# Sign bits of the split weights by a 16-bit operation with one source, and 128 small matmuls at the end of attention and MLP on one core

## The chip, the cores and the metric

The kernel runs on one core of a Trainium2 chip. The core has a matrix engine (PE; its weight loads are shown as PEld), three engines that work on up to 128 partitions at a time (DVE, ACT, POOL), and SP, whose queue here issues all transfers. The metric is the device time of one execution in microseconds; less is better.

## The reference

```python
# q, k, v: 4 batches, 8 heads, 768 positions, 64 wide; block 32, window 16
k_sum = k.reshape(B, H, 24, 32, D).max(axis=3)
v_sum = v.reshape(B, H, 24, 32, D).mean(axis=3)
local = where(abs(i - j) < 16, scale * q @ k.T, -1e9)
far   = scale * q @ k_sum.T + log(32)
a     = softmax(concat([local, far], axis=-1))
x     = (a @ concat([v, v_sum], axis=2))          # to 3072 rows x 512
h     = x @ w_in                                  # 512 -> 2048
out   = maximum(0.01 * h, h) @ w_out              # 2048 -> 512
```

Each query sees the keys nearer than 16 positions and 24 block summaries; then every row goes through a two-layer MLP. Inputs and output are fp32.

## The kernel before

**Work and tiles.** The 3072 rows are eight chunks of 384 rows (three row blocks of 128). Attention of a chunk is 12 units, one row block for one pair of heads. A unit makes scores on PE (`scores`, L328: fp32, 64 rows of contraction, 64 queries and 120 keys at a time), the lowest and the exponentials on DVE and ACT (L333, L340), normalizes on DVE, transposes on PE (`turn`, L345), copies on ACT, multiplies by the values on PE (`values`, L351), and splits the result into a rounded and a rest part `x` (hi on ACT, lo on DVE). In chunk 0 the units run singly, later in pairs; a pair's scores, values and transposes of different ages form a "group" on PE, named `s_('g', n, ...)` and `to_('g', n, ...)`. The block means of v (`vsum`) are reduced on DVE (L222) and then spread by transfers (L282); the maxima of k are reduced on DVE too (L206).

**The MLP in split precision.** Matmuls run on fp32r operands in three terms: hi by hi, lo by hi, hi by lo. For each of 16 slices f of the hidden width, `m1` (L585) makes 12 matmuls of 384 columns into `h`, ACT makes `gs` and `ghi`, DVE `glo`, and `m2` makes 9 matmuls of 512 columns (L604 to L606) into the accumulators `a`.

**The weights.** They come as 64-bit floats, since the host does no arithmetic on them, in 32 tiles of 128 by 512 (w_in and w_out of each slice). `weights` turns a tile `raw` into a hi and a lo part in six steps. `s0` (L538, DVE) shifts the low words right by 29, which leaves three mantissa bits. `s1` (L541, DVE) puts the sign bit of the high word into the low word. `s2` (ACT) scales the high word's exponent. `s3` (L547, DVE) shifts the high word left by three and ors it into the low word, which is then the fp32 value. `s4` (L550, ACT) rounds it to `win_hi` or `wout_hi`, and `s5` (L553, DVE) subtracts to `win_lo` or `wout_lo`. All of DVE's steps go over 512 elements at a step of 8 bytes, except for what the last one writes. The slices of the weights are prepared once, and all eight chunks use them.

**What sets the order.** `Plan` is a list scheduler. Every operation has an engine, a cost (for DVE `65 + 1.042 n` ns, or `65 + 0.52 n` when it is called fast), a priority (a due time, with tuned offsets in tables), and dependencies, including those of the buffers. `order` takes, engine by engine, the ready operation with the lowest priority, and the result is written out with a manual schedule: it is the order of each engine's instructions and of SP's transfers. Before PE's first MLP work, wherever the plan leaves PE idle for over 300 ns, dummy matmuls on a zero tile fill the gap (`spare`, L695).

**The end.** After the last slice three accumulators are copied out by ACT, DVE and ACT (L619, L617), and SP issues three stores of 256 KB (L622). L745 is the end of the program, at which all engines meet.

Of the kernel before, what the change touches and what calls it, by code (L numbers as in the profile page):

```python
# [8 lines left out]
F32 = mybir.dt.float32  # L9
F32R = mybir.dt.float32r  # L10
BF16 = mybir.dt.bfloat16
I32 = mybir.dt.int32
AF = mybir.ActivationFunctionType
ALU = mybir.AluOpType
AX = mybir.AxisListType
# [122 lines left out]
def ACT(n, psum=False, extra=0):  # L138
    return (51 if psum else 93) + 0.833 * n + 93 * extra


def DVE(n, fast=False):
    return 65 + (0.52 if fast else 1.042) * n
# [6 lines left out]
def build(tc, ctx, a):  # L150
    nc = tc.nc
    pool = lambda name, bufs: ctx.enter_context(tc.tile_pool(name=name, bufs=bufs))
    psum = lambda name, bufs: ctx.enter_context(tc.tile_pool(name=name, bufs=bufs, space=bass.MemoryType.PSUM))
    cst = pool("cst", 1)
    st = pool("st", 2)
    ps_acc, ps_h, ps_s, ps_t = psum("pacc", 1), psum("ph", 2), psum("pss", 1), psum("pst", 1)
# [19 lines left out]
    P = Plan()  # L176
    tl = {}
    first = {}

    def load_op(name, prio, fn, **kw):  # L180
        first[name] = P.op("SP", 550, prio, fn, **kw)
        return first[name]

    def new(tag, key, shape, dt=F32, bufs=2, src=None):
        tl[key] = (src or st).tile(shape, dt, tag=tag, name="_".join(str(x) for x in key), bufs=bufs)
        return tl[key]
# [115 lines left out]
    def place(u, at=None):  # L302
        c = min(u // UPC, NCH - 1) if at is None else at
        t, d = PLACE.get(c, (UPC * c, 1.0))
        return t + d * (u - UPC * c)
# [31 lines left out]
    def expo(u, h):  # L337
        e, m, z = tiles_of(u // 2)
        n = 2 * (u % 2) + h
        nc.scalar.activation(out=e[:, n], in_=e[:, n], func=AF.Exp, scale=-1.0, bias=m[:, n:n + 1], accum_out=z[:, n:n + 1])  # L340

# [178 lines left out]
    def weights(f, w, t):  # L520
        if w:
            hi, lo = wout_hi[:, f], wout_lo[:, f]
            shape = lambda x: x
        else:
            hi, lo = win_hi[:, :, 128 * f:128 * f + 128], win_lo[:, :, 128 * f:128 * f + 128]
            shape = lambda x: x.rearrange("p (k f) -> p k f", k=4)
        kr = ("raw", f, w)

        def load():
            nc.sync.dma_start(out=new("big", kr, [128, 1024], bufs=BIG).bitcast(I32), in_=a["w"][f, w].bitcast(I32))  # L530

        lw = lambda: tl[kr].rearrange("p (n t) -> p n t", t=2)[:, :, 0]
        hw = lambda: tl[kr].rearrange("p (n t) -> p n t", t=2)[:, :, 1]
        li = lambda: tl[kr].bitcast(I32).rearrange("p (n t) -> p n t", t=2)[:, :, 0]
        hi_i = lambda: tl[kr].bitcast(I32).rearrange("p (n t) -> p n t", t=2)[:, :, 1]

        def s0():
            nc.vector.tensor_scalar(out=li(), in0=li(), scalar1=29, scalar2=None, op0=ALU.logical_shift_right)  # L538

        def s1():  # L540
            nc.vector.scalar_tensor_tensor(out=li(), in0=hi_i(), scalar=-2 ** 31, in1=li(), op0=ALU.bitwise_and, op1=ALU.bitwise_or)  # L541

        def s2():
            nc.scalar.mul(hw(), hw(), 2.0 ** -112)  # L544

        def s3():
            nc.vector.scalar_tensor_tensor(out=li(), in0=hi_i(), scalar=3, in1=li(), op0=ALU.logical_shift_left, op1=ALU.bitwise_or)  # L547

        def s4():
            nc.scalar.copy(hi, shape(lw()))  # L550

        def s5():
            nc.vector.tensor_tensor(out=lo, in0=shape(lw()), in1=hi.bitcast(F32), op=ALU.subtract)  # L553
        o = load_op(("w", f, w), t - 0.25 * BIG, load, alloc=[("big", kr, BIG)], size=128 * 4096, rate=380.0)
        o = P.op("DVE", DVE(512, True), t + 0.05, s0, after=[o], use=[kr])
        o = P.op("DVE", DVE(512), t + 0.1, s1, after=[o], use=[kr])
        o = P.op("ACT", ACT(512), t + 0.1, s2, after=[o], use=[kr])
        o = P.op("DVE", DVE(512), t + 0.12, s3, after=[o], use=[kr])
        o = P.op("ACT", ACT(512), t + 0.3, s4, after=[o], use=[kr])
        w_op[f, w] = [o, P.op("DVE", DVE(512), t + 0.4, s5, after=[o], use=[kr])]  # L560
# [4 lines left out]
    def gnew(tag, key):  # L565
        n = turns[tag]
        turns[tag] += 1
        x = f"{tag}{n % 2}"
        if n < 2:
            gap(GGAP[n + 2 * (tag == "glo")], st, x)  # L570
        return new(x, key, [128, T], F32R, bufs=1)


    def mlp(c, f0, f1, t0):
# [13 lines left out]
        def gs(f):  # L588
            nc.scalar.activation(out=new("gs", G("gs", f), [128, T], bufs=1), in_=tl[G("h", f)][:, :T], func=AF.Prelu, alpha=0.01)  # L589

        def ghi(f):
            nc.scalar.activation(out=gnew("ghi", G("ghi", f)), in_=tl[G("h", f)][:, :T], func=AF.Prelu, alpha=0.01)  # L592

# [62 lines left out]
    for c in range(NCH):  # L656
        b, cb = divmod(c, CPB)
        for p in range(NP):
            t = place(TPC * (c * NP + p))
# [6 lines left out]
        for p in range(NP):  # L666
            t = place(TPC * (c * NP + p))
            operands(c, p, t, 0 if c else 7 - 2.5 * p)
    for f in range(NF):
        for w in range(2):  # L670
            weights(f, w, LEAD - WT + min(f, SPL) * WS + max(f - SPL, 0) * WS2 + WO * w + (W0 if f == 0 else 0))
# [4 lines left out]
    t = LEAD  # L676
# [9 lines left out]
    zero = cst.tile([128, 128], BF16, name="zero")  # L686
    nc.vector.memset(zero, 0.0)
    spare = ps_acc.tile([128, 512], F32, tag="a2", name="spare")
    with tc.manual_schedule():
        until, begun = 900.0, False  # L690
        for o in todo:
            if o["eng"] == "PE" and not begun:
                begun = o.get("mlp", False)
                while until < o["at"] - FGAP:
                    nc.tensor.matmul(spare[:, :128], zero[:, :128], zero[:, :128], start=True, stop=True)  # L695
                    until += 107 if until < WARM else 57
                until = o["at"] + o["cost"]
            o["fn"]()


def layouts(q, k, v, moe_w_in, moe_w_out):
# [47 lines left out]
```

## Time and profile before

| | |
|---|---|
| Runs (3) | 655.44, 656.45, 658.07 us; median 656.45 |
| Profiled execution | 655.79 us, its span 654.0 us |
| PE busy | 643.3 us (98%), granted clock 0.999 |
| DVE, ACT, POOL busy | 283.5, 298.4, 4.2 us |
| DMA | 58.08 MB, mean 89 GB/s |

The span runs from the first to the last instruction; what the time has beyond it lies around the program. Busy time is a mean over stages of very different kinds, so the prediction reads it by stretches. Ends of matmuls are modelled, and matmuls overlap, so that the distance between starts tells more than a matmul's own duration. A row of instructions has the engine, the line, the operation, what it writes and reads, its shape and its count; then busy us, mean ns of one, and the engine's idle time before them.

### The profile page before, as it was taken

What the parts mean: (1) busy time and instruction counts of PE and PEld (TensorE: products, weight loads), DVE (VectorE), ACT (ScalarE), POOL (GpSimd) and SP (SyncE); (2) the same over time, 40 slices, a digit from 0 to 9 for tenths busy, and PEclk for the clock granted to TensorE, in tenths of its full rate; (3) what the DMA queues carried; (4) which work ended last, traced back from release to release, by engine and by line L of the source; (5) the groups of instructions that cost most, each with busy time, mean ns of one, the idle gap of its engine ahead of it and who ended that gap; (6) DMA issues with size and microseconds to landing.
All of it is one profiled execution on the core that took longest, in us unless ns stands there. A gap on an engine that the chain in (4) does not pass through costs nothing.

```text
span 654.0 us, 11675 instructions
## 1 busy us (share of the span) xinstructions
PE 643.3 (98%) x4582; PEld 559.4 (86%) x4582; DVE 283.5 (43%) x931; ACT 298.4 (46%) x894; POOL 4.2 (1%) x10
## 2 busy tenths in 40 slices
PE   8899999999999999999999999999999999999997
PEld 5588788898888998888888888888888888889996
DVE  5999999933575212223353423242233323211111
ACT  5898776733655313444434443353443434222112
POOL 0200000000000000000000000000000000000000
PEclk9999999999999999999999999999999999999999
DMA  8977577601754000211334220020111100010001
GB/s 313 280 237 243 187 228 238 182 1 46 202 166 140 5 1 24 73 37 52 99 91 122 60 61 26 26 94 24 35 36 35 62 24 1 1 50 1 1 1 48
DMA packets 27207, 58.08 MB, mean 89 GB/s; under 512 B 3024, under 2 KB 13328, under 8 KB 27152
## 3 DMA queue, kind: packets, MB, share of 16 engines
q1 hardware_dynamic: 27152, 57.33, 28.8%
q8 instruction: 36, 0.59, 0.4%
q14 instruction: 19, 0.16, 0.1%
HBM read 48.97 MB, written 6.29 MB: 84 GB/s over the span
## 4 chain that ended last, share of the span: by engine, by line
PE 89%; DVE 5%; DMA 3%; ACT 2%; issue 1%; SPq 0%; ACTq 0%
PE h L585 39%; PE a L605 13%; PE a L604 13%; PE a L606 13%; DMA raw<-in_w_dram 1%; DMA v<-vsum 1%; ACT e L340 1%; PE spare L695 1%; DVE raw L547 1%; DVE raw L541 1%; DMA kn<-in_k_dram 1%; DVE wout_lo L553 0%; PE o L351 0%; DVE e L333 0%; DVE glo L595 0%
## 5 line engine op out<-in xcount | busy, mean ns | idle before, releaser
L585 PE MATMUL h<-x,win_hi 128*128 128x384 f32 x1024 | 263.8, 338 | 0.0
L595 DVE TENSOR_TENSOR glo<-gs,ghi 128x384 fp32r<-128x384 f32 x128 | 71.2, 557 | 285.1 <-ACT gs L589 285.0
L585 PEld LDWEIGHTS h<-x,win_hi 128*128 128x128 f32 x1024 | 186.0, 188 | 9.7 <-issue 0.2
L592 ACT ACTIVATE ghi<-h 128x384 fp32r<-128x384 f32 x128 | 62.7, 490 | 266.1 <-PE h L585 265.7
L585 PE MATMUL h<-x,win_lo 128*128 128x384 f32 x512 | 173.0, 338 | 1.0 <-DVE win_lo L553 1.0
L604 PE MATMUL a<-wout_hi,ghi 128*128 128x512 f32 x384 | 153.5, 400 | 0.0
L605 PE MATMUL a<-wout_lo,ghi 128*128 128x512 f32 x384 | 151.8, 395 | 0.0
L606 PE MATMUL a<-wout_hi,glo 128*128 128x512 f32 x384 | 151.3, 394 | 0.0
L585 PEld LDWEIGHTS h<-x,win_lo 128*128 128x128 f32 x512 | 96.0, 188 | 1.6 <-DVE win_lo L553 1.6
L606 PEld LDWEIGHTS a<-wout_hi,glo 128*128 128x128 f32 x384 | 72.2, 188 | 16.9
L605 PEld LDWEIGHTS a<-wout_lo,ghi 128*128 128x128 f32 x384 | 72.3, 188 | 11.6 <-DVE wout_lo L553 0.4
L604 PEld LDWEIGHTS a<-wout_hi,ghi 128*128 128x128 f32 x384 | 72.1, 188 | 11.6
L340 ACT ACTIVATE e<-e,m 128x120 f32<-128x120 f32 x192 | 73.9, 389 | 5.5 <-DVE m L333 5.1
L589 ACT ACTIVATE gs<-h 128x384 f32<-128x384 f32 x128 | 62.2, 486 | 1.7 <-PE h L585 1.1
L340 ACT ACTIVATION_READ_ACCUMULATOR e<-e,m 128x1 f32 x192 | 36.7, 191 | 0.0
L479 DVE TENSOR_TENSOR e<-e,z 128x480 f32<-128x480 f32 x42 | 27.5, 655 | 0.9
L273 ACT COPY k<-kn 128x288 f32<-128x288 f32 x64 | 24.4, 433 | 4.6 <-DMA kn<-in_k_dram 4.6
L544 ACT ACTIVATE raw<-raw 128x512 f32<-128x512 f32 x32 | 21.7, 691 | 9.2 <-DVE raw L541 9.1
L541 DVE SCALAR_TENSOR_TENSOR raw<-raw 128x512 int32<-128x512 int32 x32 | 22.2, 698 | 0.0
L547 DVE SCALAR_TENSOR_TENSOR raw<-raw 128x512 int32<-128x512 int32 x32 | 21.4, 684 | 0.4 <-ACT raw L544 0.3
L471 DVE TENSOR_SCALAR z<-z 128x4 f32<-128x4 f32 x42 | 7.0, 168 | 33.3 <-ACT e L340 33.3
L206 DVE TENSOR_REDUCE ksum<-kn 128x24 f32<-128x768 f32 x16 | 15.2, 948 | 8.1 <-DMA kn<-in_k_dram 8.1
(588 smaller groups left out, 493.3 us busy)
## 6 DMA issues: line engine op xcount, KB each, us to landing
raw<-in_w_dram SPq DMA_DIRECT2D x32, 512.0 KB
v<-in_v_dram SPq DMA_DIRECT2D x32, 288.0 KB
kn<-in_k_dram SPq DMA_DIRECT2D x16, 400.0 KB
k<-in_q_dram SPq DMA_DIRECT2D x32, 192.0 KB
out_dram<-out SPq DMA_DIRECT2D x21, 256.0 KB
vb<-in_vb_dram SPq DMA_DIRECT2D x12, 384.0 KB
kn<-in_k_dram SPq DMA_DIRECT2D x16, 208.0 KB
v<-vsum SPq DMA_DIRECT2D x24, 72.0 KB
```

Source lines behind the costliest of these rows:

```text
L273: nc.scalar.copy(k, x)
L340: nc.scalar.activation(out=e[:, n], in_=e[:, n], func=AF.Exp, scale=-1.0, bias=m[:, n:n + 1], accum_out=z[:, n:n + 1])
L479: nc.vector.tensor_tensor(out=e, in0=e, in1=z.unsqueeze(2).broadcast_to([128, 4, LK]), op=ALU.mult)
L541: nc.vector.scalar_tensor_tensor(out=li(), in0=hi_i(), scalar=-2 ** 31, in1=li(), op0=ALU.bitwise_and, op1=ALU.bitwise_or)
L547: nc.vector.scalar_tensor_tensor(out=li(), in0=hi_i(), scalar=3, in1=li(), op0=ALU.logical_shift_left, op1=ALU.bitwise_or)
L585: nc.tensor.matmul(h[:, :T], w[:, k, 128 * f:128 * f + 128], x[:, k], start=n == 0, stop=n == 11)
L589: nc.scalar.activation(out=new("gs", G("gs", f), [128, T], bufs=1), in_=tl[G("h", f)][:, :T], func=AF.Prelu, alpha=0.01)
L592: nc.scalar.activation(out=gnew("ghi", G("ghi", f)), in_=tl[G("h", f)][:, :T], func=AF.Prelu, alpha=0.01)
L595: nc.vector.tensor_tensor(out=gnew("glo", G("glo", f)), in0=tl[G("gs", f)], in1=tl[G("ghi", f)].bitcast(F32), op=ALU.subtract)
L604: nc.tensor.matmul(o, gh, wout_hi[:, f], start=f == f0, stop=False)
L605: nc.tensor.matmul(o, gh, wout_lo[:, f], start=False, stop=False)
L606: nc.tensor.matmul(o, gl, wout_hi[:, f], start=False, stop=f == f1 - 1)
```

## The change

Two edits. In `s1` an operation with two sources on 32-bit words becomes one with a single source on 16-bit words: it takes the upper half of the high word, keeps its top bit, and writes it to the upper half of the low word, which is zero after `s0`. The plan is given the fast cost for it. At the end, behind all planned work, PE makes 128 fp32 matmuls of a zero tile `zw` by itself in eight shapes into the two banks that `h` used; nothing reads the results. `zw` is cleared on DVE at the start.

```diff
         def s1():
-            nc.vector.scalar_tensor_tensor(out=li(), in0=hi_i(), scalar=-2 ** 31, in1=li(), op0=ALU.bitwise_and, op1=ALU.bitwise_or)
+            w16 = tl[kr].bitcast(I16).rearrange("p (n t) -> p n t", t=4)
+            nc.vector.tensor_scalar(out=w16[:, :, 1], in0=w16[:, :, 3], scalar1=-2 ** 15, scalar2=None, op0=ALU.bitwise_and)
...
         o = P.op("DVE", DVE(512, True), t + 0.05, s0, after=[o], use=[kr])
-        o = P.op("DVE", DVE(512), t + 0.1, s1, after=[o], use=[kr])
+        o = P.op("DVE", DVE(512, True), t + 0.1, s1, after=[o], use=[kr])
...
     nc.vector.memset(zero, 0.0)
     spare = ps_acc.tile([128, 512], F32, tag="a2", name="spare")
+    zw = cst.tile([128, 128], F32, name="zw")
+    nc.vector.memset(zw, 0.0)
...
             o["fn"]()
+
+        end = [ps_h.tile([128, 512], F32, tag="h", name=f"end{i}") for i in range(2)]
+        for rows, cols, n, count in ((64, 64, 120, 16), (64, 64, 88, 16), (64, 32, 88, 32), (128, 64, 64, 8), (128, 64, 32, 16), (128, 32, 32, 16),
+                                     (64, 64, 24, 16), (64, 128, 24, 8)):
+            for i in range(count):
+                r, c = i % (128 // rows), i // (128 // rows) % (128 // cols)
+                nc.tensor.matmul(end[r][cols * c:cols * c + cols, :n], zw[rows * r:rows * r + rows, :cols], zw[rows * r:rows * r + rows, :n], start=True, stop=True)
```

The new cost changes the plan, and with it the order on PE, DVE, ACT and SP as long as weights are prepared. In what follows, the line numbers after the change are one to three higher. A name's number tells buffers apart.

On DVE, the third weight tile, `raw_0_389`, before (its `s1` is L541, its `s0` stands earlier):

```order
L541 SCALAR_TENSOR_TENSOR raw_0_389<-raw_0_389 128x512
L288 COPY k_1_520<-ksum_1_177 128x6x24
L538 TENSOR_SCALAR raw_0_454<-raw_0_454 128x512
L541 SCALAR_TENSOR_TENSOR raw_1_368<-raw_1_368 128x512
L471 TENSOR_SCALAR z_619<-z_619 128x4
L541 SCALAR_TENSOR_TENSOR raw_0_454<-raw_0_454 128x512
```

And after (`raw_0_373`; `s0` is now L539, `s1` L543, `s3` L549):

```order
L539 TENSOR_SCALAR raw_0_373<-raw_0_373 128x512
L382 RECIPROCAL z_511<-z_511 128x2
L543 TENSOR_SCALAR raw_0_373<-raw_0_373 128x512
L386 TENSOR_TENSOR e_509<-e_509,z_511 128x240
L378 TENSOR_SCALAR z_511<-z_511 128x2
L539 TENSOR_SCALAR raw_0_450<-raw_0_450 128x512
L382 RECIPROCAL z_511<-z_511 128x2
L549 SCALAR_TENSOR_TENSOR raw_0_373<-raw_0_373 128x512
```

Before, this tile's sign step stood behind the four L333 of group 6, at row 122 of DVE's order; now it stands ahead of them, at row 110, and its `s3` follows at row 115, where it stood at row 133.

On PE, around the scores and transposes of group 7 (L328 and L345), before; `h_0` and `h_1` belong to the first and second slice:

```order
L328 MATMUL s_('g', 7, 1)_721<-k_1_520 64x120 x2
L328 MATMUL s_('g', 7, 1)_722<-k_1_520 64x120 x2
L345 MATMUL to_('g', 7, 1)_723<-ident,e_617 120x128 x4
L585 MATMUL h_0_605<-x_80,win_hi 128x384
L585 MATMUL h_0_605<-x_84,win_hi 128x384
L585 MATMUL h_0_605<-x_80,win_lo 128x384
L585 MATMUL h_1_759<-x_80,win_hi 128x384
```

And after, with L587 for L585, L329 for L328 and L346 for L345:

```order
L587 MATMUL h_1_717<-x_80,win_lo 128x384
L587 MATMUL h_0_598<-x_80,win_hi 128x384
L587 MATMUL h_0_598<-x_84,win_hi 128x384
L587 MATMUL h_0_598<-x_80,win_lo 128x384
L329 MATMUL s_('g', 7, 1)_738<-k_0_399 64x120 x2
L329 MATMUL s_('g', 7, 1)_739<-k_0_399 64x120 x2
L329 MATMUL s_('g', 7, 1)_738<-k_1_538 64x120 x2
L329 MATMUL s_('g', 7, 1)_739<-k_1_538 64x120 x2
L346 MATMUL to_('g', 7, 1)_740<-ident,e_660 120x128 x4
L587 MATMUL h_1_717<-x_80,win_hi 128x384
```

Nine of the 12 matmuls of the second slice and the last three of the first moved ahead of group 7; the second slice's last three stay behind it. The dummies L695 go from 154 to 150.

At PE's end, before, the program ends behind the last slice's matmuls:

```order
L605 MATMUL a_0_1_6220<-wout_lo,ghi_15_6620 128x512
L606 MATMUL a_0_1_6220<-wout_hi,glo_15_6624 128x512
L604 MATMUL a_0_2_6224<-wout_hi,ghi_15_6620 128x512
L605 MATMUL a_0_2_6224<-wout_lo,ghi_15_6620 128x512
L606 MATMUL a_0_2_6224<-wout_hi,glo_15_6624 128x512
L745 UNCONDITIONAL_BRANCH
```

After, these rows stand among the new ones (L709), where the shape goes from 64x32 tiles over 128x64 and 128x32 back to 64x64:

```order
L709 MATMUL end_6642<-zw 32x88
L709 MATMUL end_6643<-zw 32x88
L709 MATMUL end_6642<-zw 64x64 x8
L709 MATMUL end_6642<-zw 64x32 x16
L709 MATMUL end_6642<-zw 32x32 x16
L709 MATMUL end_6642<-zw 64x24
L709 MATMUL end_6643<-zw 64x24
```

Where a tile takes 64 rows of contraction, the two halves of the rows alternate and write to two banks; where it takes 128, all go to one bank. None of the new matmuls waits for anything but the last readers of the banks of `h`.

More of the change, by code (lines that the diff above doesn't have):

```diff
@@ L12 @@
 I32 = mybir.dt.int32
+I16 = mybir.dt.int16
 AF = mybir.ActivationFunctionType
```

## The prediction

> **What bounds the kernel now.** I read the page's totals and its slices first, then busy time by stretches, then who waited for whom, and last the order of time at the start and at the end.
>
> ```profile
> span 654.0 us, 11675 instructions
> PE   8899999999999999999999999999999999999997
> DVE  5999999933575212223353423242233323211111
> PE 89%; DVE 5%; DMA 3%; ACT 2%; issue 1%; SPq 0%; ACTq 0%
> L541 DVE SCALAR_TENSOR_TENSOR raw<-raw 128x512 int32<-128x512 int32 x32 | 22.2, 698 | 0.0
> L538 DVE TENSOR_SCALAR raw<-raw 128x512 int32<-128x512 int32 x32 | 13.1, 424 | 0.2 <-DMA raw<-in_w_dram 0.2
> ```
>
> ```profile
> core 0: us, PE busy (x) PEld busy (x) DVE busy (x) ACT busy (x) POOL busy (x), PEclk, DMA share, GB/s
> 16.00:24.00 8.00, 6.83 (x73) 3.08 (x74) 7.57 (x28) 5.87 (x25) 2.65 (x4) 1.00 0.99 287
> 24.00:32.00 8.00, 7.40 (x123) 5.31 (x124) 7.67 (x41) 7.48 (x32) 0.83 (x1) 1.00 0.94 268
> 32.00:44.00 12.00, 11.48 (x119) 9.81 (x117) 11.62 (x42) 11.10 (x36) 0.00 (x0) 1.00 0.76 224
> 44.00:118.00 74.00, 71.81 (x546) 61.79 (x546) 72.97 (x186) 56.33 (x142) 0.00 (x0) 1.00 0.74 226
> 118.00:650.00 532.00, 532.00 (x3589) 470.27 (x3586) 174.49 (x593) 208.58 (x632) 0.00 (x0) 1.00 0.18 53
> 650.00:654.00 4.00, 0.18 (x1) 0.00 (x0) 0.19 (x1) 0.58 (x1) 0.00 (x0) 0.82 0.53 197
> ```
>
> There are three stages. From 118 to 650 us PE is busy all the time, so nothing on DVE can move that part. From 16 to 118 DVE is busy almost without a break (72.97 of 74 us in the largest stretch), and PE has gaps or runs the dummy matmuls of L695. After 650 PE has nothing to do and the last rows leave. The change touches the second stage (L541, the sign step, 32 times) and the third (new matmuls). Only two things count: how much earlier PE becomes saturated, and whether the new matmuls outlast the end.
>
> The profiled execution took 655.79 us for a span of 654.0, so 1.8 us lie around it. The median of the runs is 656.45, or 0.66 above it. I make the sum on the span and put the difference onto the median. About 0.5%, 3.3 us, is what a measurement of this kernel can tell from no change.
>
> **The sign step.**
>
> ```profile
> 34.01 0.42 DVE L538 TENSOR_SCALAR raw<-raw 128x512 int32<-128x512 int32 x1
> 34.35 0.68 DVE L541 SCALAR_TENSOR_TENSOR raw<-raw 128x512 int32<-128x512 int32 x1
> 34.95 0.16 DVE L471 TENSOR_SCALAR z<-z 128x4 f32<-128x4 f32 x1
> ```
>
> The busy time of L541 alone, by stretches:
>
> ```profile
> 0.00:44.00 44.00, 4.52 (x6) 1.00 0.87 276
> 44.00:118.00 74.00, 14.31 (x21) 1.00 0.74 226
> 118.00:160.00 42.00, 3.41 (x5) 1.00 0.21 65
> ```
>
> L538 has one source and the same 512 elements at a step of 8 bytes; the next instruction starts 0.34 us after it. After L541, which has two sources, it starts 0.60 us later. The new step has one source and steps of 8 bytes, on 16-bit elements. No row shows a 16-bit operation, so its bounds are 0.60 (no gain) and, were it twice as fast as L538 again, 0.17. I take 0.34, since L538 is its nearest neighbour in all but the width of the element.
> The Trainium skill, "VectorE: DVE Perf Modes", section "What auto-detection actually checks", says that a single source in SBUF gives two elements a cycle, and four only if every tensor is 16-bit with a step of one. The step here is four elements, so by that page the 0.17 is out; no run here shows it yet.
>
> Each step saves 0.26 us: 6 of them by 44 us, or 1.6 us (the row's 4.52 us for six holds one slow one, which could add 0.4); 21 more by 118, another 5.5; the last 5 lie where PE is saturated, and are worth nothing. What of that reaches PE?
>
> ```profile
> PE h L585 <- DVE win_lo L553: 1.0, 2, 0.5
> PE s_('g', 14, 2)_1690 L351 <- DMA v<-vsum: 0.9, 1, 0.9
> PE t L345 <- ACT pt L396: 0.9, 1, 0.9
> PE to_('g', 11, 1)_1128 L345 <- DVE e L479: 0.8, 1, 0.8
> ```
>
> Up to 44 us DVE decides when the weights are ready, and the dummies stand in PE's way only as filling, so I take the 1.6 in full. After 44 PE has 74 - 71.81 = 2.2 us of gaps to lose, whatever DVE saves. Of these the wait for e (0.8) hangs on DVE, and the wait for vsum's transfer (0.9) starts behind DVE reductions; I take 1.3. The sum is -2.9 us. The ends are 0 (the transfers hold the start: DMA share 0.99 and 0.94 up to 32 us; ACT is next in line with 7.48 of 8 us) and -5.5 (2.6 at the start, were each step 0.17, all of the 2.2, and 0.7 of waits at matmuls that count as busy).
>
> The planner has the new price too, so it writes another order on all engines. On PE, nine matmuls of the second slice of w_in now stand ahead of the scores and transposes of group 7, which stood ahead of them before; they need win_lo of that slice, whose DVE operation moves up as well. If that comes late, the scores wait behind it, and with them DVE and ACT. Dummies go from 154 to 150, worth 0.3 us at most where nothing else waits (11 of them took 0.72 us in the chain, below). The loads on SP's queue change places by one to three; their buffers come free earlier with DVE, so they go out earlier, into transfers that are dense up to 32 us. I put the reordering at 0, between -1 and +2.
>
> ```profile
> 7.79 0.72 PE spare L695 x11
> ```
>
> The memset of zw on DVE costs nothing: DVE waits 4.9 us there for the first keys, and a memset of half as many words took 0.11 us.
>
> ```profile
> 0.82 0.11 DVE L687 MEMSET zero<- 128x64 uint32 x1 [0.82 <-PEq L739]
> 5.83 0.95 DVE L206 TENSOR_REDUCE ksum<-kn 128x24 f32<-128x768 f32 x1 [4.90 <-DMA kn<-in_k_dram]
> ```
>
> **The 128 matmuls at the end.** First the room for them.
>
> ```profile
> 649.42 1.73 SPq L622 DMA_DIRECT2D out_dram<-out  x3
> 649.54 0.40 PE L605 MATMUL a<-wout_lo,ghi 128*128 128x512 f32 x1
> 649.78 0.40 PE L606 MATMUL a<-wout_hi,glo 128*128 128x512 f32 x1
> 650.21 0.58 ACT L619 COPY out<-a 128x512 f32<-128x512 f32 x1 [0.82 <-PE a L606]
> L745 SPq EVENT_SEMAPHORE  x7: 17/28/28, 653.0 to 653.9; - x7
> L745 SPq DRAIN  x3: 7/7/7, 653.3 to 653.6; - x3
> L745 PEldq DRAIN  x2: 13/1333/2653, 647.6 to 653.6; - x2
> ```
>
> PE's queue drains at 647.6 + 2.65 = 650.2. SP waits for the last store until 653.0, works off its waits until its own drain at 653.3, and then all engines meet, 0.7 us before the end. So PE may work until 653.3 at no cost. The new matmuls start at 650.0 (649.78 and the step from the one before, 0.24), with 3.3 us of cover. What do they take? Each fp32 matmul is two instructions in the trace, so there are 256.
>
> ```profile
> 60.29 0.27 PE L328 MATMUL s_('g', 10, 1)_1036<-k 64*64 64x120 f32 x2
> 60.30 0.27 PE L328 MATMUL s_('g', 10, 1)_1037<-k 64*64 64x120 f32 x2
> 60.39 0.27 PE L328 MATMUL s_('g', 10, 1)_1036<-k 64*64 64x120 f32 x2
> 60.50 0.27 PE L328 MATMUL s_('g', 10, 1)_1036<-k 64*64 64x120 f32 x2
> 60.71 0.69 PE L351 MATMUL s_('g', 10, 1)_1036<-pt,v 120*64 120x64 f32 x16
> 61.33 0.65 PE L345 MATMUL to_('g', 10, 1)_1038<-ident,e 128*120 128x128 f32 x4
> 61.73 0.59 PE L585 MATMUL h<-x,win_hi 128*128 128x384 f32 x2
> ```
>
> In 64x64 tiles four instructions run side by side (_1037 starts 10 ns after _1036), and a round for 120 columns takes 0.10 us. L351 (128x64, two tiles) makes 16 in 0.62 us with a change of shape; without it about 0.06 a round. L345 loads 120 columns of weights for 0.10 us each (4 to the next group in 0.40). A change of shape costs 0.14: the round at 60.50 is 0.21 long in place of 0.10, and the next group's first is longer too.
>
> By shape: 64x64 with 120 columns, 8 rounds of 0.10, 0.8; with 88 columns, 8 of 0.075, 0.6; 64x32 with 88, 8 rounds if all eight tiles go together, 0.6; 128x64 with 64, 8 of 0.06, 0.5; with 32 columns, 16 rounds that the weights hold at 0.06, 0.9; 128x32, 8 of 0.03, 0.3; 64x64 with 24, 8 of 0.06, 0.5; 64x128, 8 of 0.11, 0.9. That is 5.1, and six changes of shape make 5.9 us. The low end is 4.2 (rounds by columns alone, no load in the way); the high end is L351's mean for all 256, 39 ns each, 10 us.
>
> So PE ends at 650.0 + 5.9 + 0.2 = 656.1, and then follow 0.7 us (the barrier alone) to 1.0 (SP's waits as well); with 0.9 that is 657.0, or +3.0 us. The ends are +1.3 and +7.
>
> **Sum.** +3.0 - 2.9 = +0.1 us on the profiled execution, 655.9; on the median, 656.5.
>
> **Rivals.**
> - The tail is covered. If the tiles of a round start as close as the scores' do (10 ns) in all shapes, 256 instructions at 13 ns each take 3.3 us and nothing shows; with 3.9 us won in front in place of 2.9, that is 656.5 - 3.0 - 1.0 = 652.5. For it speaks that close start; against it, the 0.10 us from round to round and the 39 ns of L351. It decides from a front gain of 3.3 us on.
> - A slow tail. If the rounds don't form over eight tiles or in the narrow shapes, L351's 39 ns makes +7: 656.5 + 4 = 660.5. In the densest 8 us of the table PE made 123 matmuls, 65 ns each, waits included; were that what it can issue in a long run, 256 take 16.6 us, and the time is 667. Sixteen in 0.62 us speak against that, unless they had been queued ahead. It decides from 36 ns an instruction on (a tail of 9.1 us).
> The Trainium skill, "TensorE: Matmul & The Clock Gate", section "Wait — 56ns, not 53.3ns?", puts the issue at about 62 ns a matmul when the sequencer decodes in software; by that, an estimate, 256 are 15.9 us. The sixteen in 0.62 us don't bear it out for short runs; no run here shows a long one.
> - The 16-bit operation isn't fast. At 0.60 us DVE saves nothing, and only the tail is left, 656.5 + 2.9 = 659.4. Since the planner then counts on time that DVE doesn't have, some waits of PE can come on top, 660.5.
> - The new order brings new waits: group 7 behind the second slice's win_lo, at 0.5 us for each such wait as in the row of win_lo. Three or four of them eat the gain: 659 to 660.
>
> **How the numbers follow.** My forecast, 653.5 to 659, has 0.57; the covered tail, with its gain, 0.17; the slow tail 0.13; the 16-bit operation at full price 0.07; the bad order 0.06. Faster by over 0.5% (under 653.2) is the second case and a sliver of the first, 0.18; slower (over 659.7) is the slow tail and half of the last two, 0.20; the rest is 0.62. The range takes in the covered tail and the price of a slow operation: 652.4 to 660.5.
>
> **What would show it.** The sign step's group should have a mean near 0.42 us, as L538 has. DVE should have visible gaps before 118 us, and PE's waits for win_lo, e and vsum should be shorter. PE's matmuls of the second slice of w_in should start some 2 us earlier than before. The tail should run from about 647 to 653 and end last in the chain. A tail under 3.3 us, or one of over 10, or a sign step of 0.68 would make me wrong, and so would a gain of over 5 us before 118.

## The result, and the profile after

The changed kernel takes 661.27 us (median of 9 runs, 660.72 to 662.80) against 656.45 for the kernel before on the same chip: a ratio of 1.0063, with a 95% interval of 1.0038 to 1.0088. It is slower by 0.6%; the forecast was 656.5 with a range up to 660.5. The ratio is not the quotient of the two medians, which is 1.0073; the nine executions of the kernel before in this comparison took 655.39 to 661.38. The profiled execution took 661.15 us for a span of 659.4 (before: 655.79 and 654.0).

From the page of the changed kernel: the head, the slices of PE and DVE, the chain by engine, and the group of the new sign step; then, from the groups on the tile `raw`, durations as minimum, median and maximum.

```profile
span 659.4 us, 12173 instructions
PE   9899899999999999999999999999999999999999
DVE  5999999913575212232254332332233233111111
PE 83%; DVE 8%; DMA 6%; ACT 2%; issue 1%; SPq 0%
L543 DVE TENSOR_SCALAR raw<-raw 128x512 int16<-128x512 int16 x32 | 23.9, 753 | 0.0
```

```profile
L539 DVE TENSOR_SCALAR raw<-raw x32: 398/429/693, 12.5 to 128.8; 128x512 int32<-128x512 int32 x32
L543 DVE TENSOR_SCALAR raw<-raw x32: 717/752/815, 13.0 to 129.8; 128x512 int16<-128x512 int16 x32
```

The sign step does not have the 0.42 us of the shift next to it. Its mean is 753 ns, where the operation that it replaces had 698. DVE stays as full as it was, and its share of the chain goes from 5% to 8%. Stretches of the changed kernel, with the columns that the prediction showed:

```profile
44.00:118.00 74.00, 69.51 (x532) 58.71 (x531) 72.26 (x188) 55.27 (x144) 0.00 (x0) 1.00 0.71 222
118.00:650.00 532.00, 532.00 (x3588) 470.33 (x3587) 173.76 (x592) 208.79 (x632) 0.00 (x0) 1.00 0.18 54
650.00:660.00 10.00, 8.37 (x266) 7.13 (x264) 0.69 (x1) 1.17 (x2) 0.00 (x0) 1.00 0.23 82
```

PE was to lose its gaps between 44 and 118 us. It lost busy time instead: 69.51 in place of 71.81 us, 2.3 us less. From 118 to 650 it is full as before, so what is lost by 118 is lost for good. What PE waited for (total, times, longest) (the first three rows are new):

```profile
PE to_('g', 12, 1)_1256 L346 <- ACT win_hi L552: 1.6, 1, 1.6
PE to_('g', 13, 2)_1586 L346 <- DVE e L480: 1.0, 1, 1.0
PE to_('g', 14, 2)_1683 L346 <- ACT ghi L594: 0.9, 1, 0.9
PE h L587 <- DVE win_lo L555: 0.8, 2, 0.6
```

And the end, with the last matmul of the second layer and the new matmuls of L709:

```profile
651.71 0.40 PE L608 MATMUL a<-wout_hi,glo 128*128 128x512 f32 x1
652.04 6.44 PE L709 MATMUL end<-zw 64*64 64x120 f32 x256
651.35 1.74 SPq L624 DMA_DIRECT2D out_dram<-out  x3
```

The last matmul of the second layer starts at 651.71 us (649.78 before): 1.9 us are lost in front. From there to the end of the span it is 7.66 us (4.23 before): 3.4 us are lost behind. Together that is the 5.4 us by which the span grew, from one profiled execution to the other.

### The profile page after: what moved, and what is told of

Same layout as the page of the kernel before. It is cut to its first block, busy times and chain, and to the rows that moved or that the text cites. A ratio compares the mean times of both kernels' runs of the same rounds, so it can differ in the third digit from the quotient of the medians.

```text
span 659.4 us, 12173 instructions
## 1 busy us (share of the span) xinstructions
PE 650.5 (99%) x4834; PEld 565.4 (86%) x4834; DVE 282.4 (43%) x932; ACT 297.6 (45%) x894; POOL 4.1 (1%) x10
## 4 chain that ended last, share of the span: by engine, by line
PE 83%; DVE 8%; DMA 6%; ACT 2%; issue 1%; SPq 0%
PE h L587 36%; PE a L606 12%; PE a L607 12%; PE a L608 12%; DMA vb<-in_vb_dram 2%; DVE raw L543 2%; DMA v<-in_v_dram 1%; DVE raw L549 1%; DMA raw<-in_w_dram 1%; DVE wout_lo L555 1%; PE end L709 1%; DVE win_lo L555 1%; DMA kn<-in_k_dram 1%; DVE raw L539 1%; DVE glo L597 1%
## 5 line engine op out<-in xcount | busy, mean ns | idle before, releaser
L587 PE MATMUL h<-x,win_hi 128*128 128x384 f32 x1024 | 263.7, 338 | 0.0
L587 PEld LDWEIGHTS h<-x,win_hi 128*128 128x128 f32 x1024 | 186.0, 188 | 9.7 <-ACT win_hi L552 0.2
L587 PE MATMUL h<-x,win_lo 128*128 128x384 f32 x512 | 173.1, 338 | 0.9 <-DVE win_lo L555 0.8
L587 PEld LDWEIGHTS h<-x,win_lo 128*128 128x128 f32 x512 | 96.0, 188 | 1.9 <-DVE win_lo L555 1.9
L480 DVE TENSOR_TENSOR e<-e,z 128x480 f32<-128x480 f32 x42 | 27.7, 659 | 0.9
L543 DVE TENSOR_SCALAR raw<-raw 128x512 int16<-128x512 int16 x32 | 23.9, 753 | 0.0
L549 DVE SCALAR_TENSOR_TENSOR raw<-raw 128x512 int32<-128x512 int32 x32 | 21.9, 693 | 0.0
```

The costliest lines, as they stand in the source:

```text
L480: nc.vector.tensor_tensor(out=e, in0=e, in1=z.unsqueeze(2).broadcast_to([128, 4, LK]), op=ALU.mult)
L543: nc.vector.tensor_scalar(out=w16[:, :, 1], in0=w16[:, :, 3], scalar1=-2 ** 15, scalar2=None, op0=ALU.bitwise_and)
L587: nc.tensor.matmul(h[:, :T], w[:, k, 128 * f:128 * f + 128], x[:, k], start=n == 0, stop=n == 11)
```

## The experiments

The first four part the change into its tail, its operation and its order. Ratios are to the kernel before on the same chip, with 95% intervals.

**1. Without the tail.** The changed kernel less `zw`, its memset and the matmuls of L709.

> The 16-bit sign step with its new price in the plan, without the 128 matmuls and their memset. The theory is that the loss has two parts that add up: 1.9 us ahead of 650 us (the last matmul of L607 starts that much later in the changed kernel) and 3.4 us behind it. It expects 658.4 us against 656.45, a ratio of 1.003, with the last matmul of the second layer starting at about 651.7 us in the trace. The rival, that the early part costs nothing and 1.9 us are scatter from one profiled execution to the next, expects 656.5. A second rival, that the tail also delays the front (its code or its PSUM buffers), expects under 657 and a start of that matmul at 649.8.

Measured: 657.79 us against 656.11, 1.0028 (1.0012 to 1.0043), that is +1.8 us. The front does lose, and by about what the traces had shown; the last matmul of the second layer starts at 651.61 us.

**2. The tail alone.**

```diff
+    zw = cst.tile([128, 128], F32, name="zw")
+    nc.vector.memset(zw, 0.0)
...
+        end = [ps_h.tile([128, 512], F32, tag="h", name=f"end{i}") for i in range(2)]
+        for rows, cols, n, count in ((64, 64, 120, 16), (64, 64, 88, 16), (64, 32, 88, 32), (128, 64, 64, 8), (128, 64, 32, 16), (128, 32, 32, 16),
+                                     (64, 64, 24, 16), (64, 128, 24, 8)):
...
```

> The kernel before with the 128 matmuls and the memset added, and the sign step as it was. The theory expects a tail of 6.4 to 6.6 us that outlasts 3.3 us of cover, so 656.45 + 3.4 = 659.9 us, a ratio of 1.005. The rival, that the matmuls lie under the stores and the loss of the changed kernel is all in the front, expects 656.5. If the memset or the code of the tail delays the start of the kernel as well, the last matmul of the second layer starts after 650.2 us and the time is over 660.5.

Measured: 659.80 us, 1.0059 (1.0038 to 1.0079), +3.9 us. The two parts add up to the whole within their intervals.

**3. The 16-bit operation in the old order.** Without the tail, and with the old price, `DVE(512)`, 599 ns, in the plan.

```diff
-        o = P.op("DVE", DVE(512, True), t + 0.1, s1, after=[o], use=[kr])
+        o = P.op("DVE", DVE(512), t + 0.1, s1, after=[o], use=[kr])
```

> The 16-bit sign step with the old price in the plan, so that the order of the instructions is that of the kernel before, and no tail. Theory A (the operation itself is slow, 0.07 us more from start to start than the one it replaced, 27 of them before PE is saturated): up to 27 x 0.07 = 1.9 us, about 658 us where DVE's time counts in full and 657 where half of it does. Theory B (the new order is what costs, since it counts on time that DVE does not have): 656.5, no change.

Measured: 656.17 against 656.11 us, 1.0006 (0.9988 to 1.0025). The operation costs nothing in this order. The expectation took the step for 0.07 us slower than the old one; it is 0.07 us faster from start to start (below, experiments 5 and 6).

**4. The old operation in the new order.** Without the tail, and the two-source step back, with the price of 331 ns.

```diff
-            w16 = tl[kr].bitcast(I16).rearrange("p (n t) -> p n t", t=4)
-            nc.vector.tensor_scalar(out=w16[:, :, 1], in0=w16[:, :, 3], scalar1=-2 ** 15, scalar2=None, op0=ALU.bitwise_and)
+            nc.vector.scalar_tensor_tensor(out=li(), in0=hi_i(), scalar=-2 ** 31, in1=li(), op0=ALU.bitwise_and, op1=ALU.bitwise_or)
```

> The two-source sign step of the kernel before (0.60 us from start to start) with the new price in the plan, so that the order is that of the changed kernel, and no tail. Theory A (the slow operation costs the 1.9 us): 656.5, or under it by some tenths where the order is good. Theory B (the order costs it): 658.4, with the waits of the changed kernel for the second slice's weights and for group 12 to 14 still there, each about 1 us.

Measured: 658.55 us, 1.0035 (1.0020 to 1.0050), +2.3 us. So the order loses the time, and not the operation. PE's new waits for groups 12 and 14 are there, that for group 13 is not:

```profile
PE to_('g', 12, 1)_1254 L346 <- ACT win_hi L551: 1.7, 1, 1.7
PE to_('g', 14, 2)_1681 L346 <- DVE e L480: 1.2, 1, 1.2
```

In the old order with the 16-bit step (experiment 3) the longest of this kind is

```profile
PE to_('g', 11, 1)_1128 L346 <- DVE e L480: 0.8, 1, 0.8
```

The releaser named for group 12 is ACT's rounding of `win_hi`, but these transposes read `ident` and `e`. The timeline of DVE in experiment 4, and then rows of ACT and PE, show when `e` came:

```profile
72.05 0.68 DVE L554 TENSOR_TENSOR win_lo<-raw,win_hi 128x512 fp32r<-128x512 f32 x1
72.65 0.68 DVE L554 TENSOR_TENSOR wout_lo<-raw,wout_hi 128x512 fp32r<-128x512 f32 x1
73.25 0.76 DVE L539 TENSOR_SCALAR raw<-raw 128x512 int32<-128x512 int32 x2
73.92 0.68 DVE L542 SCALAR_TENSOR_TENSOR raw<-raw 128x512 int32<-128x512 int32 x1
74.52 0.27 DVE L334 CUSTOM_DVE_ANT_0 e<-s_('g', 11, 1)_1164,mask 128x120 f32<-128x120 f32 x1
...
77.83 0.66 DVE L542 SCALAR_TENSOR_TENSOR raw<-raw 128x512 int32<-128x512 int32 x1
78.41 0.65 DVE L480 TENSOR_TENSOR e<-e,z 128x480 f32<-128x480 f32 x1
```

```profile
74.84 0.37 ACT L494 CAST x<-s_('g', 11, 1)_1164 128x256 fp32r<-128x256 f32 x1 [1.87 <-DVE m L334]
79.21 0.69 PE L346 MATMUL to_('g', 12, 1)_1254<-ident,e 128*120 128x128 f32 x4 [1.72 <-ACT win_hi L551]
```

Group 12's transposes read `e` from L480. L480 ends at 79.06 behind a sign step; its chain starts with L334, which starts at 74.52 behind five steps of the weights. ACT stands still for 1.87 us, put down to the wait for L334, and PE for 1.72. The five steps alone don't make the wait: in the old order (experiment 3) five stand ahead of the same L334 too, but DVE comes to it 4.2 us earlier, and the transposes follow the matmuls of L352 with no wait:

```profile
70.28 0.28 DVE L334 CUSTOM_DVE_ANT_0 e<-s_('g', 11, 1)_1126,mask 128x120 f32<-128x120 f32 x1
75.66 0.69 PE L352 MATMUL s_('g', 12, 1)_1231<-pt,v 120*64 120x64 f32 x16
76.28 0.65 PE L346 MATMUL to_('g', 12, 1)_1232<-ident,e 128*120 128x128 f32 x4
```

In the new order PE comes to L352 of this group at 76.80 us, only 1.1 us later than here. So DVE is late against PE.

**5 and 6. An operation that is fast.** One source on 32-bit words; it leaves out the OR, and with it three mantissa bits of each weight. First with the old price and order:

```diff
-            nc.vector.scalar_tensor_tensor(out=li(), in0=hi_i(), scalar=-2 ** 31, in1=li(), op0=ALU.bitwise_and, op1=ALU.bitwise_or)
+            nc.vector.tensor_scalar(out=li(), in0=hi_i(), scalar1=-2 ** 31, scalar2=None, op0=ALU.bitwise_and)
```

> The sign step as a one-source operation on 32-bit words (the sign bit of the upper word alone; it leaves out the OR, so the three lowest mantissa bits of each weight are lost), with the old price and so the old order, no tail. Theory 1: it starts its successor 0.34 us on, as the shift of L538 does, in place of 0.60, and the front gain of the prediction was right for such an operation: 656.1 - 2.9 = 653.2 us. Theory 2: in the old order the time that DVE saves goes into other waits, as the 0.07 us that the 16-bit step saves each time (0.53 against 0.60, 27 times, 1.9 us) already showed nothing: 655.5 to 656.1.

then with the new price and order:

> The same one-source 32-bit sign step (it too leaves out the three lowest mantissa bits) with the new price in the plan, so the new order, and no tail. The plan's price of 331 ns is then true. Theory 1 (the new order is bad only because the plan counts on time that DVE does not have): the waits for groups 12 to 14 go, and the time is at or under that of the same operation in the old order, 653 us. Theory 2 (this order is bad whatever the operation takes): 1.5 to 2.4 us above the same operation in the old order, 655.5 to 658.

Measured against 656.68 us: 655.00 in the old order, 0.9976 (0.9958 to 0.9995), and 655.49 in the new, 0.9978 (0.9957 to 0.9999): -1.6 and -1.4 us. The first theories expected 2.9 us, and in the new order the waits for groups 12 to 14 to go. Those waits shrink instead, for group 14 to 0.2 us and for group 12 to 0.9:

```profile
PE to_('g', 12, 1)_1254 L346 <- DVE e L480: 0.9, 1, 0.9
```

The rows of the old order show 0.33 us from this step to the next start:

```profile
62.00 0.42 DVE L541 TENSOR_SCALAR raw<-raw 128x512 int32<-128x512 int32 x1
62.33 0.69 DVE L553 TENSOR_TENSOR wout_lo<-raw,wout_hi 128x512 fp32r<-128x512 f32 x1
```

The 16-bit step, in the kernel without the tail, takes 0.53 to the next start, though it shows 0.74 as its own duration (the median of the 31 that are followed at once is 0.534):

```profile
72.96 0.74 DVE L543 TENSOR_SCALAR raw<-raw 128x512 int16<-128x512 int16 x1
73.49 0.32 DVE L334 CUSTOM_DVE_ANT_0 e<-s_('g', 11, 1)_1164,mask 128x120 f32<-128x120 f32 x1
```

| sign step, start to start | old order (599 ns) | new order (331 ns) | what the new order adds |
|---|---|---|---|
| two sources, 0.60 us | 1 | 1.0035 | 2.3 us |
| 16-bit, 0.53 us | 1.0006 | 1.0028 | 1.4 us |
| one source, 32-bit, 0.34 us | 0.9976 | 0.9978 | 0.1 us |

With an operation that takes what the plan counts on, the new order costs nothing that these runs can show; with the old operation it costs 2.3 us. Each ratio is known to some 1.0 to 1.4 us, and so the entries of the last column to some 1.0, 1.6 and 1.9 us from top to bottom: the first is clear of zero, the middle one is not by itself, and that the cost grows with the distance from the price is suggested and not shown.

**7. Ten forms in a row on DVE.** Put into the last `s5`, three times each; the eight below differ in width, step and place: an AND on words at a step of 8 bytes, one on words at unit step (`j`), four operations on halfwords at a step of 8 bytes (`h`; the first is that of the change, the third in place, the fourth a shift), and an AND on halfwords at 4 bytes and one at unit step (`b`). The other two are the 32-bit shift and the two-source step.

```diff
...
+                    V(li(), hi_i(), -2 ** 31)
...
+                    V(j[:, :512], j[:, 512:], -2 ** 31)
+                    V(h[:, :, 1], h[:, :, 3])
+                    V(h[:, :, 0], h[:, :, 2])
+                    V(h[:, :, 1], h[:, :, 1])
+                    V(h[:, :, 1], h[:, :, 3], 15, ALU.logical_shift_right)
+                    V(b[:, 0:1024:2], b[:, 1024:2048:2])
+                    V(b[:, 0:512], b[:, 512:1024])
```

> The kernel before with ten forms of one-source operations, three times each in a row on DVE, after the last weight is split (about 17 us of DVE time near 130 us; its time as a whole says nothing). Read from start to start: the 32-bit shift 0.34 us and the 32-bit AND from the upper to the lower word 0.34, the two-source step 0.60. For the 16-bit AND, theory A (16-bit elements at a step of 8 bytes go at one a cycle whatever the halfword): 0.53 for all three offsets and for the shift; at a step of 4 bytes 0.53 or 0.34, at unit step 0.34 or less. Theory B (it is the odd halfword, off the 4-byte boundary, that costs it): 0.34 for the offset that reads halfword 2 and writes halfword 0. Theory C (it is that the source is not the destination): 0.34 in place.

Measured: in the first round the 32-bit shift at a step of 8 bytes; then in the third round the 32-bit AND at unit step; the 16-bit AND from halfword 3 to 1; the AND in place; the 16-bit shift; the AND at a step of 4 bytes; the AND at unit step:

```profile
134.11 0.43 DVE L559 TENSOR_SCALAR raw<-raw 128x512 int32<-128x512 int32 x1
146.59 0.43 DVE L559 TENSOR_SCALAR raw<-raw 128x512 int32<-128x512 int32 x1
147.05 0.74 DVE L559 TENSOR_SCALAR raw<-raw 128x512 int16<-128x512 int16 x1
148.16 0.77 DVE L559 TENSOR_SCALAR raw<-raw 128x512 int16<-128x512 int16 x1
148.96 0.73 DVE L559 TENSOR_SCALAR raw<-raw 128x512 int16<-128x512 int16 x1
149.49 0.50 DVE L559 TENSOR_SCALAR raw<-raw 128x512 int16<-128x512 int16 x1
150.02 0.30 DVE L559 TENSOR_SCALAR raw<-raw 128x512 int16<-128x512 int16 x1
```

Neither the halfword, nor the operation, nor another destination than the source makes it slow: at a step of 8 bytes all 16-bit forms take 0.73 to 0.79 us, and those that the next instruction need not wait for start it 0.53 to 0.57 on. At 4 bytes they end after 0.50, at unit step after 0.30, while the 32-bit forms take 0.43 at both of their steps. So theory A holds. Instructions here often depend on the one before and wait for its end, so neither the 0.34 of the 32-bit forms nor the start-to-start time at a step of 4 bytes shows in this kernel.

**8. A tail within the cover.** Only the first three shapes, 64 matmuls.

```diff
-        for rows, cols, n, count in ((64, 64, 120, 16), (64, 64, 88, 16), (64, 32, 88, 32), (128, 64, 64, 8), (128, 64, 32, 16), (128, 32, 32, 16),
-                                     (64, 64, 24, 16), (64, 128, 24, 8)):
+        for rows, cols, n, count in ((64, 64, 120, 16), (64, 64, 88, 16), (64, 32, 88, 32)):
```

> The kernel before with the memset and only the first three shapes of the tail, 64 matmuls, 128 instructions, 2.9 us of PE by the groups of the changed kernel's trace. Theory (PE has 3.3 us of cover at the end, and only what is over it counts): 656.1, no change. Rival (any work of PE after the last row delays the end by its own length): 656.1 + 2.9 = 659. Rival (the memset or the additional code costs time at the start): 657 or more with a late start of the last matmul of the second layer.

Measured: 655.81 us against 656.68, 0.9982 (0.9963 to 1.0000). Nothing is lost. In the trace the tail ends at 652.96 us, when the last of the three stores' packets land (652.92):

```profile
650.42 2.54 PE L706 MATMUL end<-zw 64*64 64x120 f32 x128
649.74 1.73 SPq L622 DMA_DIRECT2D out_dram<-out  x3
```

**9. A tail twice as long.** Every count doubled.

```diff
-            for i in range(count):
+            for i in range(2 * count):
```

> The kernel before with every count of the tail doubled, 256 matmuls, 512 instructions. Theory: the tail runs at the same 25 ns an instruction for as long as it lasts, so 6.4 us more than the single tail, 659.8 + 6.4 = 666.2 us. Rival: a queue filled ahead hides a slower issue in the short tail; at 62 to 65 ns for each instruction beyond the first 256 the time would be 659.8 + 16 = 676.

Measured: 668.68 us against 657.04, 1.0162 (1.0125 to 1.0199). By the ratios that is 6.8 us more than with the single tail (1.0162 less 1.0059, of 656), known to some 2.8 us; in the traces the tail takes 15.77 us against 6.71 in experiment 2, 9.1 more. So the second 256 instructions take 27 to 35 ns each, above the 25 of the expectation and far below the 62 of its rival. The trace has three holes in the tail for which no wait shows, 2.3 us in all in that execution, and at the end, behind the longest of them, the granted clock (0.50, in the eighth column) is half:

```profile
PE end L707 <- issue: 2.3, 3, 1.6
664.00:667.00 3.00, 1.87 (x18) 1.75 (x18) 0.00 (x0) 0.00 (x0) 0.00 (x0) 0.50 0.00 0
```

The queue that the profile calls "instruction" moves a packet of 16 KB every 3.4 to 3.8 us during this tail; before it the packets come 26 and 17 us apart. Whether PE had no instructions in the holes is not shown.

**10 to 12. Other prices.** First the 16-bit step with the price that it really has, 534 ns, without the tail.

```diff
-        o = P.op("DVE", DVE(512, True), t + 0.1, s1, after=[o], use=[kr])
+        o = P.op("DVE", 534, t + 0.1, s1, after=[o], use=[kr])
```

> The 16-bit sign step with the price in the plan that it has on the chip from start to start, 534 ns (the kernel before counts 599, the changed one 331), and no tail. Theory P (a plan that counts on DVE time which is not there puts weight steps ahead of the softmax steps of groups 12 and 14, and that is the loss): with an honest price 655.5 to 656.2 us, no loss and perhaps some tenths won. Theory Q (any order other than the one the rest of the plan's numbers stand with loses time): over 657.3.

Measured: 657.24 against 657.04 us, 0.9990 (0.9969 to 1.0010). No loss, and no gain. Then the two-source step with 465 and with 670 ns:

```diff
-        o = P.op("DVE", DVE(512), t + 0.1, s1, after=[o], use=[kr])
+        o = P.op("DVE", 465, t + 0.1, s1, after=[o], use=[kr])
```

> The two-source step of the kernel before (0.60 us) with a price of 465 ns, half way between old and new, no tail. Theory P: half the loss of 2.4 us that the price of 331 ns brought, about 657.3. Theory Q: a loss with no relation to the price, anywhere from 656 to 659.

> The two-source step of the kernel before with a price of 670 ns, above what it takes (602 ns from start to start), no tail. Theory P: the plan counts on too little DVE time rather than too much, so no new waits: 655.5 to 656.8. Theory Q: a loss as large as that of the price of 331 ns, 657.3 or more.

Measured, against 657.04: 661.03 us, 1.0050 (1.0031 to 1.0070), at 465; 656.37 us, 0.9983 (0.9961 to 1.0005), at 670. In these runs prices below what the operation takes lose time, true and higher ones do not. But 465 was to lose half of what 331 loses, and it lost 3.3 us.

The plan computes a start for every operation. The trace's start of the sign steps, less the plan's, in us (worked out for each of the 32; the first, ninth, 17th, 25th and last are shown):

| price and operation | 1st | 9th | 17th | 25th | 32nd | time |
|---|---|---|---|---|---|---|
| 599, two sources (before) | 0.0 | 1.3 | 0.7 | 0.7 | 1.5 | 1 |
| 599, 16-bit | 0.0 | 1.2 | 0.6 | 0.3 | 0.1 | 1.0006 |
| 331, two sources | 0.6 | 2.0 | 3.7 | 7.0 | 8.6 | 1.0035 |
| 331, 16-bit (no tail) | -0.2 | 1.3 | 2.8 | 6.4 | 7.7 | 1.0028 |
| 331, one source, 32-bit | 0.3 | 1.7 | 1.6 | 2.7 | 3.3 | 0.9978 |
| 465, two sources | 0.3 | 1.6 | 2.5 | 5.6 | 5.8 | 1.0050 |
| 534, 16-bit | -0.1 | 3.0 | 3.6 | 5.4 | 6.1 | 0.9990 |
| 670, two sources | 0.4 | 2.5 | 1.8 | 2.5 | 2.7 | 0.9983 |

At 331 DVE falls behind its plan by 8 us within 32 steps (31 steps at 602 - 331 ns would be 8.4); with an operation that takes what it is priced at, or less, it stays within 3.3 us of it, except at 534. The whole plan at 331 ends 2.1 us earlier than the old one (650.7 against 652.8 by its own numbers); the chip made 2.3 us more of it. At 465 the plan itself ends 0.8 us later than at 599 (653.6), but that explains little, since the plan at 670 ends 1.5 us later (654.3) and nothing was lost there. Why 465 loses most, and how much of a loss belongs to the particular order that a price happens to give, stays open. Nor is lateness alone a measure: at the true price DVE also falls 6 us behind (in two jumps of 1.6 to 1.8 us), and the time is that of before. No version beats both kernels by more than its interval, apart from the one that drops bits.

## Why the prediction was wrong

**What bounds the kernel: right.** The time from 118 to 650 us did not change; the front and the end decided all.

**The step that failed is the price of the sign step.** The prediction took 0.34 us from start to start, from L538 as its nearest neighbour "in all but the width of the element". It is 0.534: the width, together with the step of 8 bytes, was what mattered (experiment 7). The saving is 0.07 us each and not 0.26. The upper bound of 0.60 was right as a bound, and its case stood as a rival with a chance of 0.07, at 659.4, or 660.5 if "some waits of PE" come on top; that is what happened, with a saving too small to show in the old order (experiment 3).
The Trainium skill, "VectorE: DVE Perf Modes", section "What auto-detection actually checks", was read as two elements a cycle for any single source in SBUF. The trace does not agree for 16-bit elements at a step of four (0.53 us) and agrees in direction for 32-bit ones (0.34 us for as many elements).

**What followed from it: reordering at 0.** The term had ends of -1 and +2, and with the true duration it was +1.4 (experiment 1 against 3, known to some 1.6 us), so within them. The mistake was to hold it apart from the price in the sum, though the rival of the slow operation named the link. The planner's new order is built on 331 ns; with an operation of 0.34 us the order costs 0.1 us, known to some 1.9 (experiments 5 and 6). With 0.53 the two errors are one: nothing is won on DVE, and the order counts on what was not won. The place was wrong as well: group 7 and the second slice's weights were suspected, and the time went at the transposes of groups 12 to 14, for group 12 behind `e` (experiment 4).

**The front gain of 2.9 us was too large even for a fast operation.** With 0.34 us the chip gave 1.6 (0.3 to 2.8) in the old order and 1.4 in the new. DVE's saving of 0.26 us in 27 steps is 7 us; by these medians about a fifth of it reaches PE.

**The tail: right in its mechanism, small in its size.** There is a cover: 2.54 us of matmuls cost nothing (experiment 8), 6.44 cost 3.4 in the trace, which makes the cover 3.0 us where 3.3 was taken; the runs of experiment 2 give 3.9 with an interval of 2.5 to 5.2. The term was +3.0. The tail was 6.44 us and not 5.9; the shapes with eight tiles took 0.9 instead of 0.6 for 64x32 with 88 columns, and a hole of 0.3 us stands within the 64x64 tiles with 24 columns. The 0.14 for a change of shape is 0.11 in the row that it was read from (0.21 less 0.10), which is 0.2 us over six changes and decides nothing. The rival that every instruction takes 62 to 65 ns is out: the long run of experiment 9 makes 27 to 35 ns an instruction for its second half.

**The sum with the measured terms:** +1.8 in front and +3.4 to +3.9 behind give 661.7 to 662.2 on the median of 656.45, where 661.27 was measured. With an operation as fast as assumed, 1.4 us won and the same tail, the same sum gives 658.5 to 659, inside the range.

## What to carry to other kernels

Where a planner's cost and an instruction change together, price the pair: ask what the order does if the instruction misses its cost, since an operation that keeps its old duration is then no longer neutral (+2.3 us in experiment 4). A duration taken over from a neighbour with another element width is a guess until a run with that form has shown it, and it deserves more than 7 in 100 for its slow end. Work behind the last result was free here as long as it ended about when the last store landed, and cost its excess after that; both are read from the order of time at the end.

## What the runs showed of the hardware that was not expected

- DVE takes longer over 512 halfwords at a step of 8 bytes (0.53 us to the next start, 0.75 to its own end) than over 512 words at the same step (0.34 and 0.42). The same halfwords at unit step end after 0.30.
- An operation's own duration and its start-to-start time can rank two forms in opposite ways: 753 against 698 ns by duration, 0.53 against 0.60 us by the next start. The latter is when the next instruction goes.
- Small matmuls with eight tiles side by side (64x32) started every 14 ns on average (64 in 885 ns), with 6 to 7 ns between those of one round in the first four rounds. The Trainium skill, "TensorE: Matmul & The Clock Gate", section "Wait — 56ns, not 53.3ns?", states that starts are never nearer than about 25 ns. This shape is below that; the tail as a whole has 25 ns as its mean (256 in 6.44 us).
- After the wait for group 12, the kernel without the tail ran at half the granted clock for over three microseconds (eighth column):

```profile
76.00:79.00 3.00, 1.36 (x22) 1.08 (x20) 2.94 (x9) 3.00 (x9) 0.00 (x0) 1.00 0.44 137
80.00:83.00 3.00, 3.00 (x10) 2.81 (x10) 3.00 (x6) 1.95 (x4) 0.00 (x0) 0.50 0.69 154
83.00:84.00 1.00, 1.00 (x18) 0.78 (x18) 0.85 (x2) 0.74 (x2) 0.00 (x0) 1.00 0.76 311
```

That the wait of 1.6 us brings the slow matmuls is not shown. The kernel of experiment 4 has the same drop behind a wait of 1.7 us, and the doubled tail has one behind its longest hole, but the changed kernel's profiled execution had the wait and no drop. Nor is the drop what makes the loss: three executions of the kernel without the tail had a mean clock of 0.999 or more and took 656.4 to 658.5 us, where 20 such executions of the kernel before, on the same chip, took 654.8 to 656.6.
